# A linear-attention layer with a SiLU MLP: the order of the first chunk's work, the row loads, the bonus sum and the weight transfers rearranged

## The chip, the cores and the metric

The kernel runs on one core of one Trainium2 chip. The metric is the device time of an execution in microseconds. The kernel before took 230.83 us (median of three runs, 230.15 to 231.18). The profile is that of one execution, whose span on the core was 229.3 us.

## The reference

The inputs r, k and v have the shape 4 batches x 8 heads x 768 steps x 48; w and u are 8 x 48. Per batch and head a 48 x 48 state runs over the steps, then an MLP follows:

```python
for t in range(S):
    cur = einsum('bhd,bhe->bhde', u * kt, vt)          # the bonus of the step itself
    y[:, :, t] = einsum('bhd,bhde->bhe', rt, state + cur)
    state = w * state + einsum('bhd,bhe->bhde', kt, vt)
h = x @ w_in                                            # x: y as 3072 x 384; w_in 384 x 2048
return (h * sigmoid(h)) @ w_out                         # w_out 2048 x 384
```

The bonus needs no state: for each step and head it is v times the sum over d of r*u*k.

## The kernel before, in words

The sequence is cut into 6 chunks of 128 steps, and each chunk of each of the 4 batches is a unit: unit i is chunk i // 4 of batch i % 4, 24 units in all. Units 0 to 3 are the first chunk, where the state is zero. A group is the four units of one chunk; the MLP works on a group at a time.

The steps of a unit, by the names of the functions:
- `load` (L69): three transfers (r, k, v) of 192 KB each on the row queue, which SyncE issues. Six buffers of each kind; a load waits until its buffer is free.
- `p1`: TensorE transposes r and k (L211), VectorE multiplies them by powers of w and of 1/w (rT at L213, kT at L215). From unit 4 on ScalarE casts rT to 16 bits (L218).
- `nat_v` (L163): ScalarE casts v to 16 bits (v16).
- `nat_rku` (L169, L171): GpSimd forms ku = k*u and then rku_f = r*ku. `nat_kc` (L175) forms kc, k weighted for the end of the chunk.
- `p2`: TensorE forms the products of kT and rT for the even and odd heads (L225, L227), VectorE multiplies them by the causal mask (am, L232, two instructions).
- The bonus sum over d. In units 0 to 3 it is `bonus_sum` (L193): eight pairs of ScalarE instructions, one pair per head. In the later units it is one VectorE reduction (L181, in `bonus`). GpSimd then forms vu = v * sum (L199, or L184).
- `p3y` and `p3e`: TensorE forms y from am and v16 (L250) and, after the first chunk, from the state (L247); VectorE adds vu (y16, L257).
- `sums` and `state`: TensorE forms the chunk's part of the state from kc and v16 (L266); VectorE copies or adds it (L275 to L280), and GpSimd makes the cast and the decayed copy of it (L282, L284).
- `p4`: TensorE transposes y16 (L298), ScalarE copies it to xT (L299), the input of the MLP.

The MLP is `l1` (three matmuls per tile of 128 hidden columns, L310, then SiLU on ScalarE, L313) and `l2` (four matmuls per part, L322; after four parts VectorE copies the result, L326, and the row queue stores it). An L1 tile is done for all four batches of a group (512 columns of data) or for two of them, a half.

The order on every engine is the order of the program text; there is no planner. `fill(n)` takes MLP tiles off the list `fillers` and places them between the attention steps, to fill TensorE where it would wait. At the start, before any weights are there, `spin(n)` issues n matmuls on a zeroed tile (junk) whose results are not used.

Before units 0 to 3 stand two small vectors: `to_cols` (L120, L123) turns a row of w or u into columns (a transpose and a VectorE copy), VectorE then multiplies up the powers of w (L141 to L145), and `to_rows` (L136, L138) spreads columns over all 128 partitions (four transposes and a ScalarE copy): u_bc, which ku needs, and lamC, which kc needs.

The weights w_in (win, L359) and w_out (wout, L379) come in two transfers each, 768 KB each in the kernel's 16-bit type, issued by GpSimd, between its other instructions.

PSUM tiles are named by tags: `y` has two buffers, shared by spins, y, yT, sps, cols and rows in turn; `tA` has three, for p2 and p1; `moe` three, for the MLP and p1 of units 0 to 3.

Of the kernel before, what the change touches and what calls it, by code (L numbers as in the profile page):

```python
# [8 lines left out]
FP = mybir.dt.float32  # L9
F16 = mybir.dt.float16  # L10
AF = mybir.ActivationFunctionType
# [4 lines left out]
def kernel(  # L16
# [11 lines left out]
    nc = tc.nc  # L28
# [32 lines left out]
    def unit(i):  # L61
        return divmod(i, B)

    def load(i):
        if i >= NU:
            return
        sc, b = unit(i)
        for t, src in ((rin, r), (kin, k), (vin, v)):
            nc.sync.dma_start(out=t[i % NIN][:, :, 0:D],  # L69
                              in_=src[b, :, sc * C:sc * C + C, :]  # L70
                              .rearrange("h t d -> t h d"))
# [3 lines left out]
    wrow = cst.tile([NP, 2, 64], FP)  # L75
    urow = cst.tile([NP, 2, 64], FP)
    junk = cst.tile([128, 512], F16)
    for t, src, q in ((wrow, w, nc.sync), (urow, u, nc.scalar)):
        nc.vector.memset(t[:, :, D:64], 1.0)
        q.dma_start(out=t[:, :, 0:D], in_=bass.AP(tensor=src.tensor, offset=0,  # L80
                                                  ap=[[PW, NP], [D, 2], [1, D]]))
    nc.vector.memset(junk, 0.0)
    for i in range(NIN):
        load(i)
    for t in (rin, kin):
        nc.vector.memset(t[0][:, :, D:64], 0.0)
# [25 lines left out]
    def spin(n):  # L112

        t = ps.tile([128, 512], FP, name="spin", tag="y", bufs=2)
        for _ in range(n):
            nc.tensor.matmul(t, junk[:, 0:128], junk, start=True, stop=True)

    def to_cols(row):
        t = ps.tile([128, 512], FP, name="cols", tag="y", bufs=2)
        nc.tensor.transpose(t[0:PR, 0:NP], row.rearrange("p j d -> p (j d)")[:, 0:PR],  # L120
                            ident[0:NP, 0:NP])
        c = cst.tile([PR, NP], FP, name="cols_sb", bufs=2)
        nc.vector.tensor_copy(out=c, in_=t[0:PR, 0:NP])  # L123
        return c
# [7 lines left out]
    def to_rows(dst, cols):  # L132

        t = ps.tile([128, NP, 2, 64], FP, name="rows", tag="y", bufs=2)
        for p in range(NP):
            nc.tensor.transpose(t[:, p, :, :].rearrange("t j d -> t (j d)")[:, 0:PR],  # L136
                                cols(p), ident[0:PR, 0:PR])
        nc.scalar.copy(out=dst.rearrange("t (p j) d -> t p j d", j=2), in_=t[:, :, :, 0:D])  # L138
# [21 lines left out]
    def nat_v(i):  # L160
        L = live.setdefault(i, {})
        L["v16"] = wrk.tile([128, H, D], F16, name="v16", bufs=6)
        nc.scalar.copy(out=L["v16"], in_=vin[i % NIN])  # L163

    def nat_rku(i):
        n = i % NIN
        L = live.setdefault(i, {})
        ku = wrk.tile([128, H, D], FP, name="ku")
        nc.gpsimd.tensor_tensor(out=ku, in0=kin[n][:, :, 0:D], in1=u_bc, op=ALU.mult)  # L169
        L["rku_f"] = wrk.tile([128, H, D], FP, name="rku_f")  # L170
        nc.gpsimd.tensor_tensor(out=L["rku_f"], in0=rin[n][:, :, 0:D], in1=ku, op=ALU.mult)  # L171

    def nat_kc(i):
        n = i % NIN
        nc.gpsimd.tensor_tensor(out=kc[i % NKC][:, :, 0:D], in0=kin[n][:, :, 0:D],  # L175
                                in1=lamC, op=ALU.mult)

    def bonus(i):
        L = live[i]
        rku = wrk.tile([128, H], FP, name="rku")  # L180
        nc.vector.tensor_reduce(out=rku, in_=L["rku_f"], axis=mybir.AxisListType.X,  # L181
                                op=ALU.add)
        L["vu"] = wrk.tile([128, H, D], FP, name="vu")
        nc.gpsimd.tensor_tensor(out=L["vu"], in0=vin[i % NIN],  # L184
                                in1=rku.unsqueeze(2).broadcast_to([128, H, D]),
                                op=ALU.mult)

    def bonus_sum(i):
        L = live[i]
        L["rku"] = wrk.tile([128, H], FP, name="rku")  # L190
        dump = wrk.tile([128, D], FP, name="dump")
        for h in range(H):
            nc.scalar.activation(out=dump, in_=L["rku_f"][:, h, :], func=AF.Copy,  # L193
                                 accum_out=L["rku"][:, h:h + 1])

    def bonus_vu(i):
        L = live[i]
        L["vu"] = wrk.tile([128, H, D], FP, name="vu")
        nc.gpsimd.tensor_tensor(out=L["vu"], in0=vin[i % NIN],  # L199
                                in1=L["rku"].unsqueeze(2).broadcast_to([128, H, D]),  # L200
                                op=ALU.mult)

    def p1(i, tag="tA"):
        n = i % NIN
        L = live.setdefault(i, {})
        tr = ps.tile([128, NP, C], FP, name="tr", tag=tag, bufs=3)
        tk = ps.tile([128, NP, C], FP, name="tk", tag=tag, bufs=3)
        for t, src in ((tr, rin), (tk, kin)):
            flat = src[n].rearrange("p h d -> p (h d)")
            for p in range(NP):  # L210
                nc.tensor.transpose(t[0:PR, p, :], flat[:, 128 * p:128 * p + PR], ident)  # L211
        L["rT"] = wrk.tile([PR, NP, C], FP, name="rT")
        nc.vector.tensor_tensor(out=L["rT"], in0=tr[0:PR], in1=lamR, op=ALU.mult)  # L213
        L["kT"] = wrk.tile([PR, NP, C], FP, name="kT")
        nc.vector.tensor_tensor(out=L["kT"], in0=tk[0:PR], in1=lamK, op=ALU.mult)  # L215
        if i >= B:
            L["rT16"] = wrk.tile([PR, NP, C], F16, name="rT16")
            nc.scalar.copy(out=L["rT16"], in_=L["rT"])  # L218
# [35 lines left out]
    def p3e(i):  # L254
        L = live[i]
        L["y16"] = wrk.tile([128, H, D], F16, name="y16")
        nc.vector.tensor_tensor(out=L["y16"], in0=L["y"], in1=L["vu"], op=ALU.add)  # L257
# [72 lines left out]
    def l1s(sc, b0=0, b1=B):  # L330
        return [((b1 - b0) / B, lambda ft=ft: l1(sc, ft, b0, b1)) for ft in range(NFT)]

    def l2s(sc, b0=0, b1=B):
        return [(1.0, lambda b=b, part=part: l2(sc, b, part))
                for b in range(b0, b1) for part in range(4)]
# [10 lines left out]

    uT = to_cols(urow)
    to_rows(u_bc, lambda p: uT[:, p:p + 1].broadcast_to([PR, 128]))  # L350
    for s in range(B):
        p1(s, tag="moe")
        nat_v(s)
        nat_rku(s)
        if s:
            bonus_vu(s - 1)
        if s == 2:
            for g in range(2):
                nc.gpsimd.dma_start(  # L359
                    out=win[:, :, 1024 * g:1024 * g + 1024],  # L360
                    in_=moe_w_in[:, 1024 * g:1024 * g + 1024]
                    .rearrange("(q p) n -> p q n", p=128))
        spin(2)
        if s:
            p3y(s - 1)
        p2(s, (lambda: p3e(s - 1)) if s else None)
        spin(2)
        if s:
            p4(s - 1)
        bonus_sum(s)  # L370
        if s == 1:
            to_rows(lamC, lambda p: lamCT[:, p, :])
        spin(2)
    bonus_vu(B - 1)
    p3y(B - 1)
    p3e(B - 1)
    spin(2)
    for g in range(2):
        nc.gpsimd.dma_start(  # L379
            out=wout[:, 8 * g:8 * g + 8, :],  # L380
            in_=moe_w_out[1024 * g:1024 * g + 1024, :].rearrange("(f p) n -> p f n", p=128))
    nat_kc(0)
    nat_kc(1)
    a, b_ = B, B + 1
    nat_v(a)
    nat_rku(a)
    nat_kc(2)
    nat_kc(3)
    for ft in range(4):
        l1(0, ft, 0, 2)  # L390
    p4(B - 1)
# [3 lines left out]
    def front(i):  # L395
        p1(i)
        nat_v(i)
        nat_rku(i)
        nat_kc(i)


    fillers.extend(l1s(0)[4:] + l2s(0))
    for i in range(2):
        sums(i)
        state(i)
        fill(1)
    p1(a)
    fill(1)
    for i in range(2, B):
        sums(i)  # L410
        state(i)
        fill(0.5)
    p2(a)
    bonus(a)
    nat_kc(a)
    fill(2)
    p3y(a)
    sums(a)
    p3e(a)
    state(a)  # L420
    fill(1)
    front(b_)
    fill(1)
    p4(a)
    fill(1)
    p2(b_)
    bonus(b_)
    fill(2)
    p3y(b_)
    sums(b_)  # L430
    p3e(b_)
    state(b_)
    for i in range(NIN):
        load(NIN + i)
    fill(2)
    p4(b_)
    fill(1)
    fillers[0:0] = l1s(1, 0, 2)

    front(B + 2)  # L440
    for i in range(B + 2, NU):
        sc, b = unit(i)
        rate = 1.0
        p2(i)
        fill(2 * rate)
        bonus(i)
        if i + 1 < NU:
            front(i + 1)
        if i >= NIN:
            load(i + NIN)  # L450
        fill(1 * rate)
        p3y(i)
        if sc < NCH - 1:
            sums(i)
        p3e(i)
        if sc < NCH - 1:
            state(i)
        fill(2 * rate)
        p4(i)
        fill(3 * rate)  # L460
        if b == B - 1:
            if sc == 1:
                fillers.extend(l1s(1, 2, 4) + l2s(1))
            else:
                fillers.extend(l1s(sc) + l2s(sc))
# [30 lines left out]
```

## Time and profile before

| engine | busy, us | share of the span |
|---|---|---|
| TensorE matmul | 211.3 | 92% |
| GpSimd | 118.4 | 52% |
| VectorE | 117.2 | 51% |
| ScalarE | 103.5 | 45% |

The shares are means over stages that differ. The profile gives four more views that matter here: busy time by stretch; waits, each with the waiting instruction, the one it waited for, the sum in us, the number and the longest; the timeline, with start, duration, engine, line, operation, output and inputs, and in brackets the idle time before; and the chain of waits, followed back from the last instruction. Matmuls are pipelined, so a group of n has a length of n gaps plus one latency. The releaser of a wait is inferred.

### The profile page before, as it was taken

Reading aid. Unit: us, or ns where it says so; the run is one execution under the profiler, and the core shown is the slowest. Engines: PE = TensorE matmul, PEld = TensorE weight load, DVE = VectorE, ACT = ScalarE, POOL = GpSimd, SP = SyncE. Lnnn points to the kernel's source line nnn. Section 1 sums busy time; section 2 is a strip of 40 time slices with the busy share of each in tenths; the row PEclk is TensorE's granted clock in tenths of the full one; section 3 lists DMA queues with packets and bytes.
Section 4 is the critical chain, followed back from the end, with each engine's and each line's share of the span. In section 5 each row is a group of like instructions: output and inputs, shape, how many; then the busy total and the mean of one; then the engine's idle time right before and its main releaser. Section 6 shows DMA issues by size and latency. Waiting matters only on the chain.

```text
span 229.3 us, 4655 instructions
## 1 busy us (share of the span) xinstructions
PE 211.3 (92%) x1778; PEld 139.3 (61%) x1778; DVE 117.2 (51%) x238; ACT 103.5 (45%) x256; POOL 118.4 (52%) x154
## 2 busy tenths in 40 slices
PE   7698858869789999999999999999999999999993
PEld 2475525455677678677656767666776567654551
DVE  6545534934644585377636656743775365440020
ACT  2355666516473236421488202767213863129500
POOL 8281729965780865574857458625734553410000
PEclk9999999979999999999999999999999999999999
DMA  4997598999940755163762354631012000210011
GB/s 96 214 194 151 87 190 105 188 196 206 175 99 3 172 122 123 37 137 95 168 118 46 64 137 103 137 69 37 36 37 70 3 0 0 71 42 26 3 69 69
DMA packets 81262, 22.32 MB, mean 97 GB/s; under 512 B 75352, under 2 KB 80472, under 8 KB 81240
## 3 DMA queue, kind: packets, MB, share of 16 engines
q1 hardware_dynamic: 78348, 18.88, 37.9%
q0 software_dynamic: 2880, 3.15, 8.8%
q8 instruction: 14, 0.23, 0.4%
q14 instruction: 8, 0.07, 0.1%
q10 hardware_dynamic: 12, 0.00, 0.0%
HBM read 20.45 MB, written 4.72 MB: 110 GB/s over the span
## 4 chain that ended last, share of the span: by engine, by line
PE 74%; POOL 7%; issue 6%; SPq 5%; DVE 3%; ACT 2%; DMA 1%; POOLq 0%; DVEq 0%
PE ops L322 28%; PE hps L310 24%; PE ae L225 9%; SPq L69 5%; PE tr L211 4%; PE tk L211 3%; PE sps L266 2%; POOL kc L175 2%; PE y L250 2%; DMA kin<-in_k_dram 1%; PE yT L298 1%; PE y L247 1%; POOL rku_f L171 1%; ACT gT L313 1%; POOL vu L199 1%
## 5 line engine op out<-in xcount | busy, mean ns | idle before, releaser
L310 PE MATMUL hps<-xT,win 128*128 128x512 f16 (+1 forms) x348 | 71.8, 345 | 3.6 <-ACT gT L313 2.6
L313 ACT ACTIVATE gT<-hps 128x512 f16<-128x512 f32 (+1 forms) x116 | 58.8, 524 | 27.6 <-PE hps L310 25.6
L322 PE MATMUL ops<-wout,gT 128*128 128x384 f16 x384 | 70.0, 326 | 0.0
L184 POOL TENSOR_TENSOR vu<-vin,rku 128x384 f32<-128x384 f32 x20 | 16.6, 830 | 62.5 <-DVE rku L181 62.5
L310 PEld LDWEIGHTS <-win 128*128 128x128 f16 x348 | 32.5, 99 | 27.0 <-issue 5.5
L322 PEld LDWEIGHTS <-gT 128*128 128x128 f16 x384 | 35.8, 98 | 21.4
L232 DVE TENSOR_TENSOR am<-ae,maskM 128x512 f16<-128x512 f32 x24 | 16.6, 692 | 50.5 <-PE ao L227 50.5
L218 ACT CAST rT<-rT 112x512 f16<-112x512 f32 x20 | 12.4, 618 | 50.7 <-DVE rT L213 50.7
L225 PE MATMUL ae<-rT,kT 48*128 48x128 f32 x192 | 28.6, 291 | 1.7 <-DVE kT L215 1.6
L326 DVE COPY osb<-ops 128x384 f32<-128x384 f32 x24 | 13.3, 555 | 33.0 <-PE ops L322 32.5
L225 PEld LDWEIGHTS ae<-rT,kT 48*128 48x128 f32 x192 | 23.9, 193 | 9.1 <-issue 5.9
L227 PE MATMUL ao<-rT,kT 48*128 48x128 f32 x192 | 28.6, 291 | 0.0
L169 POOL TENSOR_TENSOR ku<-kin,u_bc 128x384 f32<-128x384 f32 x24 | 24.1, 1006 | 4.2 <-ACT u_bc L138 4.2
L171 POOL TENSOR_TENSOR rku_f<-rin,ku 128x384 f32<-128x384 f32 x24 | 24.1, 1002 | 1.9
L227 PEld LDWEIGHTS ao<-rT,kT 48*128 48x128 f32 x192 | 23.9, 193 | 0.0
L175 POOL TENSOR_TENSOR kc<-kin,lamC 128x384 f16<-128x384 f32 x24 | 23.9, 1001 | 0.0
L299 ACT COPY xT<-yT 128x384 f16<-128x384 f16 x24 | 11.4, 476 | 24.7 <-PE yT L298 24.7
L213 DVE TENSOR_TENSOR rT<-tr,pi 112x512 f32<-112x512 f32 x24 | 16.6, 690 | 11.3 <-PE tr L211 11.2
L257 DVE TENSOR_TENSOR y<-y,vu 128x384 f16<-128x384 f32 x24 | 13.3, 553 | 7.7 <-POOL vu L199 4.1
L215 DVE TENSOR_TENSOR kT<-tk,pi 112x512 f32<-112x512 f32 x24 | 16.3, 681 | 0.3 <-PE tk L211 0.2
L232 DVE TENSOR_TENSOR am<-ao,maskM 128x512 f16<-128x512 f32 x24 | 16.3, 680 | 0.0
L211 PE MATMUL tk<-ident,kin 128*112 128x128 f32 x96 | 15.3, 285 | 0.0
(62 smaller groups left out, 224.9 us busy)
## 6 DMA issues: line engine op xcount, KB each, us to landing
rin<-in_r_dram SPq DMA_DIRECT2D x24, 192.0 KB, 2.9
kin<-in_k_dram SPq DMA_DIRECT2D x24, 192.0 KB, 3.6
vin<-in_v_dram SPq DMA_DIRECT2D x24, 192.0 KB, 3.6
out_dram<-osb SPq DMA_DIRECT2D x24, 192.0 KB, 1.9
win<-in_moe_w_in_dram POOLq DMA_DIRECT2D x2, 768.0 KB, 9.0
wout<-in_moe_w_out_dram POOLq DMA_DIRECT2D x2, 768.0 KB, 9.8
wrow<-in_w_dram SPq DMA_DIRECT2D x1, 1.5 KB
urow<-in_u_dram ACTq DMA_DIRECT2D x1, 1.5 KB
```

The lines of the kernel that those rows point to most:

```text
L169: nc.gpsimd.tensor_tensor(out=ku, in0=kin[n][:, :, 0:D], in1=u_bc, op=ALU.mult)
L171: nc.gpsimd.tensor_tensor(out=L["rku_f"], in0=rin[n][:, :, 0:D], in1=ku, op=ALU.mult)
L175: nc.gpsimd.tensor_tensor(out=kc[i % NKC][:, :, 0:D], in0=kin[n][:, :, 0:D], in1=lamC, op=ALU.mult)
L184: nc.gpsimd.tensor_tensor(out=L["vu"], in0=vin[i % NIN], in1=rku.unsqueeze(2).broadcast_to([128, H, D]), op=ALU.mult)
L211: nc.tensor.transpose(t[0:PR, p, :], flat[:, 128 * p:128 * p + PR], ident)
L213: nc.vector.tensor_tensor(out=L["rT"], in0=tr[0:PR], in1=lamR, op=ALU.mult)
L225: nc.tensor.matmul(ae[:, p, :], L["kT"][0:D, p, :], L["rT"][0:D, p, :], start=True, stop=True)
L227: nc.tensor.matmul(ao[:, p, :], L["kT"][64:PR, p, :], L["rT"][64:PR, p, :], start=True, stop=True)
L232: nc.vector.tensor_tensor(out=am, in0=a, in1=maskM.unsqueeze(1).broadcast_to([128, NP, C]), op=ALU.mult)
L310: nc.tensor.matmul(hps, win[:, q, ft * 128:(ft + 1) * 128], xts[sc][:, q, b0:b1, :].rearrange("p b t -> p (b t)"), start=(q == 0), stop=(q ...
L313: nc.scalar.activation(out=gts[sc][:, ft, b0 * C:b1 * C], in_=hps, func=AF.Silu)
L322: nc.tensor.matmul(ops, gts[sc][:, ft, b * C:(b + 1) * C], wout[:, ft, :], start=(ft == 0), stop=(ft == NFT - 1))
```

## The change

It does five things.

1. The row of u is no longer loaded from ScalarE's queue. The row queue now carries w, then r and k of unit 0, then u, then v of unit 0. Unit 0's transposes are put ahead of u's `to_cols` and `to_rows`, which run between rT and kT of unit 0 (the argument `mid` of `load` and of `p1`).
2. The bonus sum of units 0 to 3 goes from ScalarE to one VectorE reduction, as in the later units, placed after the masks of the unit. `nat_rku` is split into `nat_ku` and `nat_rk`, and vu of the unit before is placed between them on GpSimd. y16 of the unit before is placed ahead of both masks, not between them.
3. The first weight matrix comes in three transfers (512, 512 and 1024 columns), the second in two as before, and kc of unit 0 goes ahead of the latter. Two groups of spins change in number, and one at the end of units 0 to 3 is gone.
4. Units 4 and 5 are ordered anew: their v16 cast is placed behind SiLUs, the state sums of units 0 to 3 are spread among their steps, and the bonus is placed earlier.
5. The list of fillers for this stretch holds only group 0's L1 tiles; the halves of group 1 and group 0's L2 parts are appended afterwards, and two places to fill are put before unit 6's p2.

The diff, cut to its core:

```diff
+    load_row(wrow, w)
+    load(0, mid=lambda: load_row(urow, u))
+    for i in range(1, NIN):
         load(i)
...
     def bonus_sum(i):
         L = live[i]
         L["rku"] = wrk.tile([128, H], FP, name="rku")
-        dump = wrk.tile([128, D], FP, name="dump")
-        for h in range(H):
-            nc.scalar.activation(out=dump, in_=L["rku_f"][:, h, :], func=AF.Copy,
-                                 accum_out=L["rku"][:, h:h + 1])
+        nc.vector.tensor_reduce(out=L["rku"], in_=L["rku_f"], axis=mybir.AxisListType.X,
+                                op=ALU.add)
...
         nc.vector.tensor_tensor(out=L["rT"], in0=tr[0:PR], in1=lamR, op=ALU.mult)
+        if mid:
+            mid()
...
-    uT = to_cols(urow)
-    to_rows(u_bc, lambda p: uT[:, p:p + 1].broadcast_to([PR, 128]))
+    def to_cols_u():
+        t = to_cols(urow)
+        spin(1)
+        to_rows(u_bc, lambda p: t[:, p:p + 1].broadcast_to([PR, 128]))
+
     for s in range(B):
-        p1(s, tag="moe")
+        p1(s, tag="moe", mid=to_cols_u if s == 0 else None)
         nat_v(s)
-        nat_rku(s)
+        nat_ku(s)
         if s:
             bonus_vu(s - 1)
+        nat_rk(s)
         if s == 2:
-            for g in range(2):
-                nc.gpsimd.dma_start(
-                    out=win[:, :, 1024 * g:1024 * g + 1024], ...
+            for c0, c1 in ((0, 512), (512, 1024), (1024, 2048)):
+                nc.gpsimd.dma_start(out=win[:, :, c0:c1], ...
-        spin(2)
         if s:
             p3y(s - 1)
-        p2(s, (lambda: p3e(s - 1)) if s else None)
+            p3e(s - 1)
+        spin(3)
+        p2(s)
+        bonus_sum(s)
         spin(2)
         if s:
             p4(s - 1)
-        bonus_sum(s)
...
     bonus_vu(B - 1)
     p3y(B - 1)
     p3e(B - 1)
-    spin(2)
+    nat_kc(0)
     (the two transfers of the second weight matrix)
-    nat_kc(0)
-    nat_kc(1)
-    nat_v(a)
-    nat_rku(a)
-    nat_kc(2)
-    nat_kc(3)
+    nat_ku(a)
+    nat_rk(a)
+    for i in range(1, B):
+        nat_kc(i)
     (L1 tiles 0 to 3 in halves, with unit 3's p4 between, as before)
...
-    fillers.extend(l1s(0)[4:] + l2s(0))
+    fillers.extend(l1s(0)[4:])
```

The order of units 4 and 5 after that, with a = 4 and b = 5, was: sums and state of 0 and 1, each with a fill; p1(a); sums and state of 2 and 3; p2(a), bonus(a), kc(a); p3y(a), sums(a), p3e(a), state(a); p1, v16, ku, rk and kc of b; p4(a); p2(b), bonus(b); p3y(b), sums(b), p3e(b), state(b); p4(b); with 14 fills among them. It is now:

```
p1(a) fill(1) v16(a) sum(a) vu(a) sums+state(0) fill(1) p2(a) fill(1) sums+state(1) fill(1)
p3y(a) p3e(a) kc(a) sums+state(2) fill(1) sums+state(3) p1(b) ku(b) rk(b) fill(1) p4(a)
sums+state(a) fill(1) p2(b) sum(b) vu(b) kc(b) fill(2) v16(b) fill(1) p3y(b) p3e(b)
sums+state(b) (loads of units 6 to 11) fill(2) p4(b) p1(6) ... fill(2)
```

The loop over units 6 to 23 is as before, but for y16 being placed ahead of the state sums in the text.

More of the change, by code (lines that the diff above doesn't have):

```diff
@@ L62, in unit, with load @@
         return divmod(i, B)
-    def load(i):
+    def load(i, mid=None):
         if i >= NU:
@@ L68, in load @@
         for t, src in ((rin, r), (kin, k), (vin, v)):
+            if t is vin and mid:
+                mid()
             nc.sync.dma_start(out=t[i % NIN][:, :, 0:D],
@@ L77, with load_row @@
     junk = cst.tile([128, 512], F16)
-    for t, src, q in ((wrow, w, nc.sync), (urow, u, nc.scalar)):
+    nc.vector.memset(junk, 0.0)
+    for t in (wrow, urow):
         nc.vector.memset(t[:, :, D:64], 1.0)
[L80 to L83, printed above, removed]
+    def load_row(t, src):
+        nc.sync.dma_start(out=t[:, :, 0:D], in_=bass.AP(tensor=src.tensor, offset=0,
+                                                        ap=[[PW, NP], [D, 2], [1, D]]))
+    load_row(wrow, w)
+    load(0, mid=lambda: load_row(urow, u))
+    for i in range(1, NIN):
         load(i)
@@ L163, in nat_v, with nat_ku, nat_rk @@
         nc.scalar.copy(out=L["v16"], in_=vin[i % NIN])
-    def nat_rku(i):
-        n = i % NIN
+    def nat_ku(i):
         L = live.setdefault(i, {})
-        ku = wrk.tile([128, H, D], FP, name="ku")
-        nc.gpsimd.tensor_tensor(out=ku, in0=kin[n][:, :, 0:D], in1=u_bc, op=ALU.mult)
+        L["ku"] = wrk.tile([128, H, D], FP, name="ku")
+        nc.gpsimd.tensor_tensor(out=L["ku"], in0=kin[i % NIN][:, :, 0:D], in1=u_bc,
+                                op=ALU.mult)
+    def nat_rk(i):
+        L = live[i]
         L["rku_f"] = wrk.tile([128, H, D], FP, name="rku_f")
-        nc.gpsimd.tensor_tensor(out=L["rku_f"], in0=rin[n][:, :, 0:D], in1=ku, op=ALU.mult)
+        nc.gpsimd.tensor_tensor(out=L["rku_f"], in0=rin[i % NIN][:, :, 0:D], in1=L["ku"],
+                                op=ALU.mult)
     def nat_kc(i):
@@ L176, in nat_kc @@
                                 in1=lamC, op=ALU.mult)
[L178 to L186, printed above, removed]
     def bonus_sum(i):
@@ L201, in bonus_vu, with p1 @@
                                 op=ALU.mult)
-    def p1(i, tag="tA"):
+    def p1(i, tag="tA", mid=None):
         n = i % NIN
@@ L213, in p1 @@
         nc.vector.tensor_tensor(out=L["rT"], in0=tr[0:PR], in1=lamR, op=ALU.mult)
+        if mid:
+            mid()
         L["kT"] = wrk.tile([PR, NP, C], FP, name="kT")
@@ L345, in fill @@
             f()
-    uT = to_cols(urow)
-    to_rows(u_bc, lambda p: uT[:, p:p + 1].broadcast_to([PR, 128]))
+    def to_cols_u():
+        t = to_cols(urow)
+        spin(1)
+        to_rows(u_bc, lambda p: t[:, p:p + 1].broadcast_to([PR, 128]))
     for s in range(B):
-        p1(s, tag="moe")
+        p1(s, tag="moe", mid=to_cols_u if s == 0 else None)
         nat_v(s)
-        nat_rku(s)
+        nat_ku(s)
         if s:
             bonus_vu(s - 1)
+        nat_rk(s)
         if s == 2:
-            for g in range(2):
-                nc.gpsimd.dma_start(
-                    out=win[:, :, 1024 * g:1024 * g + 1024],
-                    in_=moe_w_in[:, 1024 * g:1024 * g + 1024]
-                    .rearrange("(q p) n -> p q n", p=128))
-        spin(2)
+            for c0, c1 in ((0, 512), (512, 1024), (1024, 2048)):
+                nc.gpsimd.dma_start(out=win[:, :, c0:c1],
+                                    in_=moe_w_in[:, c0:c1]
+                                    .rearrange("(q p) n -> p q n", p=128))
         if s:
             p3y(s - 1)
-        p2(s, (lambda: p3e(s - 1)) if s else None)
+            p3e(s - 1)
+        spin(3)
+        p2(s)
+        bonus_sum(s)
         spin(2)
@@ L397, in front @@
         nat_v(i)
-        nat_rku(i)
+        nat_ku(i)
+        nat_rk(i)
         nat_kc(i)
-    fillers.extend(l1s(0)[4:] + l2s(0))
[L403 to L406, printed above, removed]
+    fillers.extend(l1s(0)[4:])
     p1(a)
     fill(1)
[L409 to L412, printed above, removed]
-    p2(a)
-    bonus(a)
-    nat_kc(a)
-    fill(2)
-    p3y(a)
+    nat_v(a)
+    bonus_sum(a)
+    bonus_vu(a)
+    sums(0)
+    state(0)
+    fill(1)
+    p2(a)
+    fill(1)
+    sums(1)
+    state(1)
+    fill(1)
+    p3y(a)
+    p3e(a)
+    nat_kc(a)
+    sums(2)
+    state(2)
+    fill(1)
+    sums(3)
+    state(3)
+    p1(b_)
+    nat_ku(b_)
+    nat_rk(b_)
+    fill(1)
+    p4(a)
     sums(a)
-    p3e(a)
     state(a)
     fill(1)
-    front(b_)
-    fill(1)
[L424 to L428, printed above, removed]
+    p2(b_)
+    bonus_sum(b_)
+    bonus_vu(b_)
+    nat_kc(b_)
+    fill(2)
+    nat_v(b_)
+    fill(1)
     p3y(b_)
+    p3e(b_)
     sums(b_)
-    p3e(b_)
     state(b_)
@@ L436 @@
     p4(b_)
-    fill(1)
-    fillers[0:0] = l1s(1, 0, 2)
+    fillers.extend(l1s(1, 0, 2) + l2s(0))
     front(B + 2)
+    fill(2)
     for i in range(B + 2, NU):
         sc, b = unit(i)
-        rate = 1.0
         p2(i)
-        fill(2 * rate)
-        bonus(i)
+        fill(2)
+        bonus_sum(i)
+        bonus_vu(i)
         if i + 1 < NU:
@@ L450 @@
             load(i + NIN)
-        fill(1 * rate)
+        fill(1)
         p3y(i)
+        p3e(i)
         if sc < NCH - 1:
             sums(i)
-        p3e(i)
-        if sc < NCH - 1:
             state(i)
-        fill(2 * rate)
+        fill(2)
         p4(i)
-        fill(3 * rate)
+        fill(3)
         if b == B - 1:
```

## The prediction

> **What bounds the kernel now.** I read the busy times by stretch first, then the waits inside the stretches that are not full, then single lines of the timeline. The stretches (columns: start and end, length, then busy us and count for TensorE, its weight loads, VectorE, ScalarE, GpSimd, then granted TensorE clock, DMA share, GB/s):
>
> ```profile
> 14.00:31.50 17.50, 14.15 (x142) 9.42 (x141) 10.26 (x17) 9.48 (x48) 8.11 (x9) 1.00 0.80 145
> 31.50:60.40 28.90, 22.57 (x182) 14.62 (x181) 15.45 (x35) 15.45 (x41) 20.59 (x24) 0.94 1.02 176
> 60.40:75.00 14.60, 13.50 (x142) 10.87 (x143) 7.36 (x14) 7.46 (x22) 7.82 (x10) 1.00 0.40 81
> 75.00:200.00 125.00, 124.83 (x1125) 84.57 (x1123) 71.25 (x136) 55.56 (x112) 72.26 (x86) 1.00 0.35 81
> ```
>
> From 75 us on TensorE has no gap (124.83 of 125), so nothing that the change does there can gain. All it can win lies before 75: in the first 31.5 us (the attention of units 0 to 3, a chain of latencies in which spins fill TensorE) and from 31.5 to 60.4, where TensorE is busy 22.57 of 28.9 us at clock 0.94. The waits of 31.5 to 75, then of the first 31.5 us, say who makes it wait:
>
> ```profile
> POOL vu L199 <- ACT dump L193: 4.4, 1, 4.4
> DVE y L257 <- POOL vu L199: 4.1, 1, 4.1
> PEld L266 <- POOL kc L175: 3.7, 4, 1.9
> PE hps L310 <- ACT gT L313: 2.4, 3, 1.8
> PE sps L266 <- POOL kc L175: 2.2, 2, 1.8
> ```
>
> ```profile
> POOL vu L199 <- ACT dump L193: 7.2, 3, 5.1
> DVE rT L213 <- PE tr L211: 4.4, 4, 2.0
> POOL ku L169 <- ACT u_bc L138: 4.2, 1, 4.2
> PE rows L136 <- DVE cols_sb L123: 1.9, 1, 1.9
> ```
>
> ScalarE's bonus sum (dump) is what GpSimd waits for in every unit of the first chunk: 11.6 us in four waits. Behind vu stand, on GpSimd's queue, the weight transfers and kc; behind y16 stands the last transpose that the MLP needs. Single lines of the timeline (start, duration):
>
> ```profile
> 16.67 0.37 PE L225 MATMUL ae<-rT,kT 48*128 48x128 f32 x1 [0.31 <-DVE kT L215]
> 17.86 0.69 DVE L232 TENSOR_TENSOR am<-ae,maskM 128x512 f16<-128x512 f32 x1 [1.25 <-PE ao L227]
> 33.75 0.83 POOL L199 TENSOR_TENSOR vu<-vin,rku 128x384 f32<-128x384 f32 x1 [4.38 <-ACT dump L193]
> 36.13 1.47 PE L310 MATMUL hps<-xT,win 128*128 128x256 f16 x12 [0.57 <-ACT xT L299]
> 48.04 0.54 PE L266 MATMUL sps<-v,kc 128*112 128x96 f16 x4 [1.84 <-POOL kc L175]
> 60.40 0.37 PE L225 MATMUL ae<-rT,kT 48*128 48x128 f32 x1 [1.01 <-DVE kT L215]
> ```
>
> The last is p2 of unit 6, my yardstick: when it starts, TensorE has done units 4 and 5, twelve whole L1 tiles of group 0 and two L2 parts (1.3 us). In the new order it will have done the same, with four half L1 tiles (4 x 0.33 = 1.3 us) in place of the two parts. So the shift of this instruction is the gain.
>
> **What the skill says.** "TensorE: Matmul & The Clock Gate", Part 1: half clock by default, full clock after one busy window of about 3.4 us, half again after an idle one, windows free-running. The trace agrees in kind: f32 matmul pairs come every 0.21 us until 13.3 and every 0.11 us from 16.9; after the 1.84 us gap at 48.04 four transposes take 0.85 us instead of 0.44, until about 51.7. "DMA: Bandwidth & Descriptors", "Issuing engines are not separate DMA queues": another issuing engine saves only sequencer time. Here the u issue costs ScalarE 1.24 us at 0.81, with nothing waiting behind it, so moving it is worth nothing by itself. "GPSIMD Engine Reference", 4.1: a sum along the free axis belongs on VectorE; the trace: 0.54 us there (L181) against 8 pairs every 0.367 = 2.9 us on ScalarE (11.89 to 14.80 for unit 0).
>
> **Part by part.** *u third on the row queue, inside p1(0).* Before, TensorE did cols(u) at 6.0 and waited 1.9 us for its copy, which stood behind the powers of w on VectorE (ending 8.02); only then rows (8.15) and unit 0's transposes (8.95). Now the transposes follow the second five spins at 6.0 and end by 7.75 (0.215 each at half clock); rT 8.02 to 8.71, cols copy 0.15, kT to 9.5 (before 11.59). Rows start 8.95. Before, no landing times are shown for the first loads; r issued at 1.71 with the median 2.9 lands at 4.6, k at 2.37 + 3.6 = 6.0, u in v's old place (2.99 + 3.6 = 6.6) before 7.75. Nothing waits by this. v moves one issue (0.65 us) and has room until 9.6.
> Clock: TensorE is now busy from 1.2 to 8.35, so by the skill full clock comes at 8 at the latest instead of 13.6. If so, rows, spin(3) and p2(0) run fast and the first mask product (am) starts at 11.3; if not, rows 0.85, spins 1.28 and p2 with its 2.12 to am put it at 13.2 (before 13.76). The bounds on this are 0 and 1.9 us; since no row shows the landings, I take the middle, 0.95.
>
> *Bonus sum on VectorE.* Adds 4 x about 0.5 us to VectorE, takes 2.9 us per unit off the chain. Stage now: rT and kT 1.29, to p2 0.05, p2 to am 1.20 (16.67 to 17.86), two am 1.22, sum 0.46: 4.2 us from rT to rT, VectorE-bound; before 5.7 and 5.0 (15.33, 21.05, 26.04). GpSimd needs per stage ku 1.0 + vu 0.83 + rk 1.0 = 2.9, hidden. y16(s-1) lies under p2(s): vu is ready 0.95 after the sum, before kT ends. Spins (3 + 2 + 2, 1.5 us) lie in TensorE's waits. Stage 1 adds 0.5 for the rows of lamC.
> With the later clock: first am 13.2, sum to 14.9, rT at 14.9, 19.65, 23.9; the last am ends 27.7, sum 28.2, vu(3) 28.25 to 29.05, y16(3) at 29.1. Three weight issues (3 x 0.85) on GpSimd at 21.1 to 23.7 hold vu(2), and so y16(2), by 0.4 us; counted. From y16 to the second group of L1 halves was 34.61 to 36.13 = 1.52: they start at 30.62 against 36.13, 5.5 us earlier.
>
> *Weights in 3 + 2.* First L1 now needs only 512 columns. Issued at 19.3 to 21.1; the 768 KB piece took 7.6 us to land, so the small one lands between 4.8 (an estimate: the fixed 2 us that "DMA: Bandwidth & Descriptors", Anatomy of one DMA, gives, plus half of the other 5.6) and 7.6 later: 24 to 28.7, needed 26.3 to 28.2. I take no wait; bound 0 to 2.4. The second piece (needed at 31 to 33) and third (needed by 37) are safe by the 10.4 us of the slower old piece.
>
> *Units 4 and 5 and the states.* After 30.62: halves 1.3, transposes to 32.83; VectorE then runs without a gap: rT, kT to 33.8, sum(4) (product ready 34.0 on GpSimd behind kc(0), two wout issues 1.8, ku, rk) to 34.6, state 0 (four copies, 1.3) to 35.9, am 37.2, state 1 38.5, y16(4) 39.0, states 2 and 3 to 41.6, rT, kT to 42.85, state 4 to 43.5; p2(5) on TensorE 42.9, am 44.1 to 45.4, sum 45.85; GpSimd vu(5) 46.7, kc(5) 47.7. TensorE's sums(5) at 47.75, then two L1 (1.3), yT, transposes of unit 6 (0.88), four halves (1.3): p2(6) at 51.7. Gaps left: 0.85 us at 37.7 (sums(2) wants the PSUM buffer of state 1) and 1.35 us at 46.4 (kc(5)); the wait of p3y(5) for v16(5), now behind two SiLUs, ends at 46.5 inside the latter. 60.40 - 51.7 = 8.7 us. This includes the loss of the old 1.84 us gap and the slow 3.5 us behind it.
>
> *Loads of units 6 to 11* wait for kc(0) (36.3 to 37.3 before, 30.05 at the latest now). Before, from the wout issue at 34.5 to the end of unit 7's k issue (44.05 + 3.56) were 13.1 us; the same from 30.1 gives 43.2, landing by 47, against p1(7) after 51. Hidden.
>
> *Fill after unit 6.* Before, 61.5 to 71 was paced by SiLU: the chain alternates 0.50 of hps with 0.39 of gT. About 12.25 us of TensorE work took 14.6 from 60.4, a loss of 2.35. Four of sixteen halves now come before p2(6), with ScalarE idle. Between 0 and 2.35 saved; I take 0.8.
>
> Sum: 8.7 + 0.95 + 0.8 = 10.45; 230.83 - 10.45 = **220.4 us**.
>
> **Rivals.** *Weights or a late landing at the start* (0.15): the small piece lands in 7.6 us or more because rows of units 4 and 5 (issued to 18.1, DMA share 1.03 in 10 to 20 us) are still moving, or u or k lands after 7.75. Costs 2.4 there, and the 0.95 is gone with a gap at 6: 220.4 + 3.4 = 223.8. For it: 7.6 is the only size shown. Against: the old piece had another beside it.
> *Clock falls in the new gaps* (0.15): 1.35 us idle at 46.4 against 1.84 before, which cost half speed for 3.5 us, 1.8 us of work: 222.2 to 222.5. Against: the 1.77 us gap at 32.6 brought no fall.
> *Gain paid back at the clock* (0.05), the other side: with no early pause TensorE's clock would stay at the 0.94 of 31.5 to 60.4: 6% of 172 us is 10.3, the whole gain, and two more half-speed windows of 1.7 make 234. Against: 1.00 through 150 gapless us.
>
> **How the numbers follow.** The forecast has 0.65. Its own spread: clock 0 to 1.9 (about plus or minus 1), fill 0 to 2.35 (plus 0.8, minus 1.5), so 217.9 to 222.2; waits in a hand-made walk are more likely missed than invented. The upper end takes in both middle rivals: 218 to 225. Faster than 0.5%: forecast and both middle rivals, 0.94; same 0.02; slower 0.04.
>
> **What would show it.** Stages of about 4.2 us between rT starts of units 1 to 3; full clock near 8 us; no L193; second L1 halves near 30; gap before sums(5) about 1.3; p2(6) near 50 to 52; from there TensorE full and everything shifted alike. Wrong if L1 waits for a weight piece, if VectorE's sum stalls on GpSimd's product in each stage, or if units 6 and 7 wait for their rows.

## The result, and the profile after

The changed kernel took 219.49 us (median of four runs, 219.48 to 221.1) against 230.49 us before, a ratio of 0.9539 (95% interval 0.9491 to 0.9586). The forecast was 220.4, with a range of 218 to 225.

The busy times of the changed kernel in four stretches (span 219.4 us; columns as before: start and end, length, busy us and count of TensorE, weight loads, VectorE, ScalarE, GpSimd, clock, DMA share, GB/s):

```profile
0.00:14.00 14.00, 11.10 (x50) 5.85 (x51) 8.32 (x30) 4.07 (x9) 7.79 (x25) 0.88 0.84 167
30.45:52.25 21.80, 18.90 (x170) 12.80 (x169) 14.68 (x34) 12.58 (x27) 19.52 (x24) 1.00 1.09 183
60.00:75.00 15.00, 15.00 (x145) 10.72 (x144) 9.73 (x19) 2.63 (x6) 7.84 (x10) 1.00 0.45 103
75.00:200.00 125.00, 124.83 (x1098) 83.05 (x1096) 67.61 (x127) 57.75 (x115) 66.29 (x79) 1.00 0.31 73
```

The second is the stretch of units 4 and 5, from the second L1 halves to p2 of unit 6. The same stretch in the kernel before:

```profile
36.13:60.40 24.27, 20.61 (x166) 13.34 (x166) 14.89 (x34) 11.35 (x23) 18.20 (x22) 0.93 1.09 186
```

It is 2.5 us shorter. TensorE's idle time in it fell only from 3.7 to 2.9 us; the other 1.7 us are busy time, since a part of the same work ran at half clock before (0.93 on the mean) and none of it does now. TensorE is full from 60 us on, not from about 71. Behind 75 us nothing changed: 124.83 of 125 in both kernels. TensorE's waits from 28 to 75 us in the changed kernel:

```profile
PE sps L267 <- DVE st L281: 1.0, 2, 0.8
PE hps L311 <- ACT gT L314: 0.8, 2, 0.6
PE sps L267 <- POOL kc L186: 0.7, 1, 0.7
PE y L251 <- ACT v L170: 0.4, 1, 0.4
```

The waits for kc fell from 2.2 to 0.7 us and those for SiLU (gT) from 2.4 to 0.8; new are 1.0 us for a PSUM buffer that a state copy holds and 0.4 us for the v16 cast that now stands behind SiLUs. The yardsticks of the prediction, from the timeline:

```profile
13.01 0.69 DVE L233 TENSOR_TENSOR am<-ae,maskM 128x512 f16<-128x512 f32 x1 [3.50 <-PE ao L228]
14.67 0.68 DVE L212 TENSOR_TENSOR rT<-tr,pi 112x512 f32<-112x512 f32 x1
19.51 0.69 DVE L212 TENSOR_TENSOR rT<-tr,pi 112x512 f32<-112x512 f32 x1 [0.56 <-PE tr L210]
23.71 0.68 DVE L212 TENSOR_TENSOR rT<-tr,pi 112x512 f32<-112x512 f32 x1
30.45 1.47 PE L311 MATMUL hps<-xT,win 128*128 128x256 f16 x12 [0.57 <-ACT xT L300]
47.33 0.41 PE L267 MATMUL sps<-v,kc 128*112 128x96 f16 x4 [0.71 <-POOL kc L186]
52.25 0.37 PE L226 MATMUL ae<-rT,kT 48*128 48x128 f32 x1
```

The second L1 halves start at 30.45 (36.13 before), p2 of unit 6 at 52.25 (60.40 before), 8.15 us earlier; the span is 9.9 us shorter, so 1.7 us more come behind p2(6). This is the trace of the execution that took 221.1 us; the other three took 219.5. Where the 1.6 us between them lie, the first experiment shows.

### The profile page after: what moved, and what is told of

It is laid out like the page before. It is cut to its first block, busy times and chain, and to the rows that moved or that the text cites. A ratio compares the mean times of both kernels' runs of the same rounds, so it can differ in the third digit from the quotient of the medians.

```text
span 219.4 us, 4605 instructions
## 1 busy us (share of the span) xinstructions
PE 207.8 (95%) x1781; PEld 137.7 (63%) x1781; DVE 118.5 (54%) x242; ACT 92.7 (42%) x192; POOL 118.9 (54%) x155
## 4 chain that ended last, share of the span: by engine, by line
PE 75%; POOL 7%; DVE 5%; SPq 4%; issue 3%; ACT 2%; DMA 2%; DVEq 0%; POOLq 0%
PE ops L323 29%; PE hps L311 24%; PE ae L226 9%; PE tr L210 4%; SPq L71 4%; PE tk L210 3%; PE sps L267 2%; POOL rku_f L181 2%; DMA vin<-in_v_dram 2%; PE y L251 1%; PE yT L299 1%; PE y L248 1%; POOL vu L198 1%; DVE rT L212 1%; POOL ku L175 1%
## 5 line engine op out<-in xcount | busy, mean ns | idle before, releaser
L311 PE MATMUL hps<-xT,win 128*128 128x512 f16 (+1 forms) x348 | 70.5, 342 | 1.5 <-ACT gT L314 0.9
L198 POOL TENSOR_TENSOR vu<-vin,rku 128x384 f32<-128x384 f32 x24 | 19.9, 829 | 64.5 <-DVE rku L192 63.0
L311 PEld LDWEIGHTS <-win 128*128 128x128 f16 x348 | 32.1, 98 | 24.1 <-issue 2.5
L226 PEld LDWEIGHTS ae<-rT,kT 48*128 48x128 f32 x192 | 23.9, 193 | 9.8 <-issue 7.1
L228 PEld LDWEIGHTS ao<-rT,kT 48*128 48x128 f32 x192 | 23.9, 193 | 0.0
L186 POOL TENSOR_TENSOR kc<-kin,lamC 128x384 f16<-128x384 f32 x24 | 23.9, 999 | 0.0
L123 PE MATMUL spin<-junk 128*128 128x512 f16 x39 | 13.6, 463 | 1.3 <-DVE wrow L82 1.3
```

Source lines behind the costliest of these rows:

```text
L198: nc.gpsimd.tensor_tensor(out=L["vu"], in0=vin[i % NIN], in1=L["rku"].unsqueeze(2).broadcast_to([128, H, D]), op=ALU.mult)
L226: nc.tensor.matmul(ae[:, p, :], L["kT"][0:D, p, :], L["rT"][0:D, p, :], start=True, stop=True)
L228: nc.tensor.matmul(ao[:, p, :], L["kT"][64:PR, p, :], L["rT"][64:PR, p, :], start=True, stop=True)
L311: nc.tensor.matmul(hps, win[:, q, ft * 128:(ft + 1) * 128], xts[sc][:, q, b0:b1, :].rearrange("p b t -> p (b t)"), start=(q == 0), stop=(q ...
```

## Experiments

The kernel before was timed again beside the experiments. Its fastest execution took 228.16 or 228.17 us each time, so times of different experiments are compared directly here.

**The changed kernel again.**

> The changed kernel once more, for a second trace. Clock theory: its shorter executions (219.5 against 221.1) are those in which TensorE keeps full clock through the 1.6 us gap before u's rows, so a trace with span near 217.8 shows p2(0) at full rate and the first mask product near 11.4 instead of 13.0, and a later course that is the same but shifted by 1.6. Rival: the shorter executions save their 1.6 us later, in the fillers or at the row loads, and the first mask product is at 13.0 in them too.

219.49 us (five executions at 219.45 to 219.51, one at 221.07); the trace has the span 217.8. From its timeline, u's rows, the spins behind them and the first mask product; then the first two of these in the trace of 219.4 us shown above:

```profile
9.06 0.57 PE L143 MATMUL rows<-ident,cols_sb 112*128 112x112 f32 x4 [0.92 <-DVE cols_sb L130]
9.47 0.81 PE L123 MATMUL spin<-junk 128*128 128x512 f16 x3
11.40 0.69 DVE L233 TENSOR_TENSOR am<-ae,maskM 128x512 f16<-128x512 f32 x1 [1.89 <-PE ao L228]
```

```profile
9.06 0.62 PE L143 MATMUL rows<-ident,cols_sb 112*128 112x112 f32 x4 [1.64 <-DVE cols_sb L130]
9.48 1.49 PE L123 MATMUL spin<-junk 128*128 128x512 f16 x3
```

Three spins take 0.81 or 1.49 us: TensorE runs at full or at half clock here, and the first mask product comes at 11.40 or 13.01. All later yardsticks are shifted by the same 1.6 us (second halves 28.84, p2(6) 50.63). The clock theory holds, but the gap in front of the rows is not the same in the two traces: 0.92 us where the clock stays, 1.64 us where it falls.

**More spins in front of u's rows.**

```diff
-        spin(1)
+        spin(5)
         to_rows(u_bc, lambda p: t[:, p:p + 1].broadcast_to([PR, 128]))
```

> The changed kernel with five spins instead of one between u's columns and rows (added: four matmuls whose results nobody uses). Clock theory: TensorE is idle for 0.9 instead of 1.6 us before the rows, full clock is not lost again, and all executions take 219.4 or less, none 221.1; the first mask product at 11.4 in every trace. Rival: the fall of the clock does not depend on this gap, and one in six still takes 221; or the spins, if run at half clock, push the rows back and the time rises to 220.

219.41 us, all six between 219.39 and 219.42. With the gap shortened (0.70 us in the trace) no execution takes 221 us. This trace and that of 219.4 us make a close pair, since in both the granted clock became full at 6.0 us. The next two stretches of 3.41 us, first in the trace of 219.4 us, then in this one (columns as above, the clock is the third from the end):

```profile
6.03:9.44 3.41, 1.77 (x14) 1.31 (x13) 3.11 (x8) 1.28 (x4) 0.00 (x0) 1.00 1.04 205
9.44:12.86 3.42, 3.42 (x21) 2.12 (x19) 0.07 (x1) 1.30 (x3) 2.50 (x3) 0.50 1.12 223
```

```profile
6.01:9.42 3.41, 2.71 (x19) 1.67 (x18) 3.10 (x9) 1.28 (x4) 0.00 (x0) 1.00 1.02 202
9.42:12.84 3.42, 3.42 (x32) 2.32 (x30) 1.59 (x4) 1.30 (x3) 2.60 (x3) 1.00 1.02 204
```

This also explains an oddity of the pair above. In the trace where the clock falls, full clock had come earlier (unit 0's eight transposes ended near 7.0 instead of 7.7), but rows are pinned to 9.06 by a copy on VectorE. So the sooner TensorE is quick, the longer it idles, 1.64 against 0.92 us, and then the clock falls back.

The length of the gap is not the whole of it. In the traces of three versions below that keep the single spin, the gap was 1.36 us (the old fillers), 1.45 us (the first weight matrix in two transfers) and 1.53 us (the old order of units 4 and 5), and the clock stayed. In a fourth, the old order inside the stages, it was even 2.23 us, and the spins behind it still ran at full clock:

```profile
9.07 0.57 PE L143 MATMUL rows<-ident,cols_sb 112*128 112x112 f32 x4 [2.23 <-DVE cols_sb L130]
9.47 0.81 PE L123 MATMUL spin<-junk 128*128 128x512 f16 x3
```

In that trace full clock had come at 4.67 us. Where the clock fell in the first 60 us of a trace, it was half for 3.41 us (four traces) or for 6.83 us (one), so it seems to be set anew every 3.41 us. Counted from 4.67, one such step ends at 8.08, inside the gap, and leaves 1.24 us of it in one step and 0.99 us in the next; the gap of 1.64 us lay wholly in one (6.03 to 9.44). That the idle share of a step decides fits this pair, but is not shown: no run moved a gap against the steps on purpose, and a gap of 1.84 us that lay wholly in one step was passed over in a trace below.

**The bonus sum back on ScalarE.**

```diff
-        nc.vector.tensor_reduce(out=L["rku"], in_=L["rku_f"], axis=X, op=ALU.add)
+        dump = wrk.tile([128, D], FP, name="dump")     # units 0 to 3
+        for h in range(H):
+            nc.scalar.activation(out=dump, in_=L["rku_f"][:, h, :], func=AF.Copy,
+                                 accum_out=L["rku"][:, h:h + 1])
```

> The changed kernel with the bonus sum of units 0 to 3 back on ScalarE. Chain theory: a stage becomes sum 2.9 + vu 0.83 + rk 1.0 = 4.8 us on the ScalarE-GpSimd loop against 4.2 to 4.4 on VectorE, so unit 3's y16 comes about 2 us later and the time is 221.5 to 222.5. Rival (order theory): with ku, vu and rk in the new order the ScalarE sum starts right after rk and lies beside the masks, so at most 0.5 us is lost: 219.5 to 220.

224.03 us, 4.5 us more than the changed kernel: the chain theory's direction, but twice its size. Lines of its timeline:

```profile
17.14 0.24 ACT L198 ACTIVATE dump<-rku_f 128x48 f32<-128x48 f32 x1 [1.49 <-POOL rku_f L181]
19.95 0.46 ACT L306 COPY xT<-yT 128x384 f16<-128x384 f16 x1
20.46 0.59 PE L123 MATMUL spin<-junk 128*128 128x512 f16 x2 [2.93 <-ACT xT L306]
21.44 1.06 PE L216 MATMUL tk<-ident,kin 128*112 128x128 f32 x4
```

The expectation looked only at who waits for the sum. Behind it on ScalarE's queue stands the copy of yT to xT, which frees a PSUM buffer; TensorE's next spins wait for that buffer, 2.93 us, unit 2's transposes stand behind the spins, and after the wait they run at half clock (1.06 for four). In the kernel before, the sum stood behind that copy, so this wait is one of this pairing of old sum and new order. How the 4.5 us divide between this wait, the half clock behind it and the wait of vu was not separated: no run puts the copy ahead of the sum in the new order.

**The VectorE sum in the kernel before**, the same edit the other way around, and nothing else.

> The kernel before with this one edit, the bonus sum of units 0 to 3 as one VectorE reduction. Chain theory: vu(1) comes 2.6 us earlier, and unit 3's y16 about 2.5 us earlier, so 227.5 to 228.5. Rival A (the sum is the whole gain of the head): y16(3) 5 us earlier, 225 or less. Rival B (order theory: the old order, with y16 between the masks and vu behind rk, holds the stage): less than 1 us, above 229.5.

226.43 us against 230.84 (ratio 0.9843, 0.9789 to 0.9896), below the range of the chain theory. The medians differ by 4.4 us; the ratio stands for 3.6, since both kernels scatter by about 2 to 3 us. y16(3) came at 32.07 against 34.61, 2.54 us earlier as the chain theory had it, and the second halves at 33.93 (2.2 earlier). In the trace p2(6) was even 4.0 us earlier: the 1.84 us gap before the sums of unit 4 was there as before, but this time without half clock behind it:

```profile
45.70 0.41 PE L264 MATMUL sps<-v,kc 128*112 128x96 f16 x4 [1.84 <-POOL kc L175]
46.59 0.60 PE L209 MATMUL tr<-ident,rin 128*112 128x128 f32 x4
```

The same transposes took 1.06 in the kernel before. So some 1.8 us of these 4.0 are the clock and not the sum. At the start the clock worked the other way: half up to 16.4 us here, up to 14.0 in the trace of the kernel before, and unit 3's rT came 0.34 us later; from there to y16(3) the sum saved 2.9 us.

**The old order inside the stages of units 0 to 3**, with the sum on VectorE.

```diff
-        if s:
-            bonus_vu(s - 1)
         nat_rk(s)
+        if s:
+            bonus_vu(s - 1)
...
-            p3e(s - 1)
         spin(3)
-        p2(s)
-        bonus_sum(s)
+        p2(s, (lambda: p3e(s - 1)) if s else None)
         spin(2)
         if s:
             p4(s - 1)
+        bonus_sum(s)
```

> The changed kernel with the old order inside the stages of units 0 to 3 (vu of the unit before behind rk on GpSimd, y16 of the unit before between the two masks), but the sum still on VectorE. Order theory: y16 between the masks adds 0.5 us to VectorE's chain of each stage and holds back the transpose of y and so the next unit's transposes on TensorE: periods of 4.8 to 5.2 instead of 4.2 to 4.8, 1.5 to 2.5 us in all: 221 to 222. Rival: with the sum off ScalarE the order is indifferent, since VectorE has the same work: within 0.4 us of 219.5.

221.62 us, all within 0.02: 2.1 us slower. Periods from rT to rT are 5.7 and 5.0 us (13.07, 18.79, 23.78) against 4.8 and 4.2, and in each of the three stages TensorE waits 0.7 us for y16; the first two:

```profile
16.81 0.34 PE L299 MATMUL yT<-ident,y 128*128 128x128 f16 x3 [0.71 <-DVE y L258]
22.53 0.34 PE L299 MATMUL yT<-ident,y 128*128 128x128 f16 x3 [0.70 <-DVE y L258]
```

These periods are those of the kernel before (15.33, 21.05, 26.04), and with the VectorE sum in the kernel before they were no shorter (15.41, 21.39, 26.38). So the sum alone does not shorten the stage; it takes its 2.5 us off the end, where unit 3's y16 waits for it. Nor does the new order alone: with the sum on ScalarE it had periods of 8.9 and 5.4 us (12.81, 21.68, 27.11). It takes both. The edit moves vu and y16 at once, and which of the two counts was not separated.

**u's part undone.**

```diff
-    load(0, mid=lambda: load_row(urow, u))
+    nc.scalar.dma_start(out=urow[:, :, 0:D], in_=(u, as in the kernel before))
+    load(0)
...
-        p1(s, tag="moe", mid=to_cols_u if s == 0 else None)
+        p1(s, tag="moe")          # and u's to_cols and to_rows ahead of the loop, without spin
```

> The changed kernel with u's part undone: u on ScalarE's queue, its columns and rows ahead of unit 0's transposes. Chain theory: the first mask product comes at 13.8 as in the kernel before, 0.7 to 2 us later than in the changed kernel by the state of the clock, and all behind it shifts: 220.2 to 221.5. Rival: GpSimd's ku and rk of unit 0 set the pace, and u_bc comes 0.4 us earlier here, so no loss or a small gain: 219 to 219.6.

221.07 us, 1.6 us slower. rows wait 1.96 us again, unit 0's transposes start at 8.94 instead of 5.8, the first mask product comes at 12.83, earlier than expected, since full clock came at 11.0 us in this trace and at 14.0 in that of the kernel before. The chain theory holds; that u_bc is ready earlier buys nothing.

**The first weight matrix in two transfers.**

```diff
-            for c0, c1 in ((0, 512), (512, 1024), (1024, 2048)):
+            for c0, c1 in ((0, 1024), (1024, 2048)):
```

> The changed kernel with the first weight matrix in two transfers of 1024 columns. Weights theory: the first piece lands 7.6 us after its issue near 19.2, at 26.8, and the first L1 half (at 26.2 in the trace of 217.8 us) waits up to 0.7 us; but y16(3) holds the second halves in any case, so at most 0.3 us is lost, and GpSimd saves one issue of 0.8 us: 219.2 to 219.8. Rival: the pieces are needed, since a landing near 30 us would hold both groups of halves: 221 or more.

220.3 us (219.94 to 221.08), 0.8 us slower, more than the 0.3 expected; in the trace, which is that of the fastest execution, 0.5. The wait is there and has the size expected of it, but y16(3), which comes when it did, does not cover all of it: unit 3's transpose of y stands behind the late halves on TensorE, and the second halves start at 29.40 against 28.84.

```profile
27.08 1.49 PE L311 MATMUL hps<-xT,win 128*128 128x256 f16 x12 [0.75 <-DMA win<-in_moe_w_in_dram]
29.40 1.47 PE L311 MATMUL hps<-xT,win 128*128 128x256 f16 x12 [0.67 <-ACT xT L300]
```

**The old fillers**, everything else as changed.

```diff
-    fillers.extend(l1s(0)[4:])
+    fillers.extend(l1s(0)[4:] + l2s(0))
...
-    fillers.extend(l1s(1, 0, 2) + l2s(0))
+    fill(2)
+    fillers[0:0] = l1s(1, 0, 2)
     front(B + 2)
-    fill(2)
```

> The changed kernel with only the filler list as before: L2 parts of group 0 fill ahead of unit 6, and the sixteen halves of group 1 come together behind its p2. Pacing theory: SiLU then paces the halves, and the 1.7 us that the changed kernel gains behind p2(6) are lost: 221.0 to 221.4. Rival: these 1.7 us come from other waits (row loads, kc) and the time stays within 0.3 us of 219.5; or L2 parts placed at 48 us wait for the second weight matrix (landing near 44) and it costs more.

221.35 us (median; two of six at 222.9, with a granted clock of 0.992 where the others have 0.997 to 1.000), 1.9 us slower. p2(6) starts at 50.77 against 50.63, so all of it is lost behind. The halves come in one run of sixteen and are paced by SiLU; the sets of twelve take 1.8 us instead of 1.5:

```profile
51.87 1.79 PE L311 MATMUL hps<-xT,win 128*128 128x256 f16 x12
56.29 1.77 PE L311 MATMUL hps<-xT,win 128*128 128x256 f16 x12 [0.50 <-ACT gT L314]
```

**The old order of units 4 and 5**, with the old fillers. The edit puts back the block from unit 4's ku to unit 6, as listed under the change.

> The changed kernel with the old order of units 4 and 5 and the old filler list. If the order itself is worth what the walk gave (gaps before the sums, and the half-clock stretch behind the 1.84 us gap), 24.3 us from the second halves to p2(6) instead of 21.8, and 1.7 us behind it: 223.2 to 223.8. Rival: the half-clock stretch was chance, and without it the old order takes 22.5 (as in the kernel before with the VectorE sum): 221.5 to 222.2.

223.66 us (single executions from 221.99 to 225.27), 4.2 us slower, of which 1.9 are the fillers. The old gap and the half clock behind it are back:

```profile
40.75 0.61 PE L267 MATMUL sps<-v,kc 128*112 128x96 f16 x4 [1.84 <-POOL kc L186]
42.43 1.06 PE L210 MATMUL tr<-ident,rin 128*112 128x128 f32 x4
```

From the second halves (28.83) to p2(6) (52.91) it takes 24.1 us, as in the kernel before (24.3); the new order takes 21.8. Most of the 2.3 us beside the fillers is the clock. The single execution at 222.0 had a granted clock of 1.000; the four near 223.6 had 0.991 or 0.992, and that at 225.3 had 0.985. So without half clock the old order costs 0.6 us (222.0 against 221.35), as the rival had it, and the half clock, which five of six executions met, costs 1.7 us. No trace of the execution at 222.0 was kept.

**kc ahead of vu in the kernel before**, the gap alone.

```diff
-    bonus(a)
     nat_kc(a)
+    bonus(a)
```

> The kernel before with one edit, kc(4) ahead of vu(4) on GpSimd, so that the 1.84 us wait of TensorE for kc(4) shrinks to about 0.3. If the wait costs its length and the half clock behind it (1.9 us more), 227.0 to 227.8; if the wait alone, 229.2; if TensorE catches up in the fillers behind it, no change.

227.75 us against 230.07 (ratio 0.9913, 0.9877 to 0.9949). In its trace the wait is 0.23 us and p2(6) starts at 57.03, 3.4 us earlier, of which 0.3 come from before the second halves. So wait and half clock together cost 3.1 us in the trace. The medians differ by 2.3 and the ratio stands for 2.0 (1.2 to 2.8), between the wait alone (1.6) and both, as they should if only some executions of the kernel before lose the clock there; that share was not measured.

**A version with both gaps shortened**: the five spins, and for unit 5 what the last experiment does for unit 4.

```diff
-        spin(1)
+        spin(5)
...
-    bonus_vu(b_)
     nat_kc(b_)
-    fill(2)
-    nat_v(b_)
+    bonus_vu(b_)
     fill(1)
+    nat_v(b_)
+    fill(2)
```

> The changed kernel with the five spins, with kc(5) ahead of vu(5) on GpSimd and the v16 cast of unit 5 one filler earlier. It should end the waits of sums(5) for kc(5) (0.7 us) and of y(5) for v16(5) (0.4 us) on TensorE, which has no slack from there on: 218.2 to 218.5 against 219.4. Rival: vu(5) comes 0.8 us later, so y16(5) and the state of unit 5 take the place of the waits and nothing is gained.

218.38 us (218.37 to 218.41), 1.1 us less than the changed kernel, 1.0 less than with the five spins alone, and the lowest of all; ratio to the kernel before 0.9504 (0.9471 to 0.9537). The wait for kc is 0.24 us and that for v16 is gone; y16(5) did not take its place.

## Why the prediction was right

**What bounds.** That only the time before 75 us could give anything held: 124.83 of 125 us busy behind it in both kernels.

**Stages of 4.2 us.** Forecast rT at 14.9, 19.65, 23.9 and second halves at 30.62, for the later clock; measured 14.67, 19.51, 23.71 and 30.45 in the trace that has that clock. The periods, forecast at 4.75 in stage 1 and 4.2 behind it, were measured at 4.84 and 4.20, and the chain named for them was right: rT, kT, the products, the masks and the sum follow each other, with VectorE waiting only 0.6 to 0.8 us at a time for TensorE. What the prediction put under the heading of the sum rests on two things by the experiments, the sum on VectorE and the order inside the stage: undoing the order alone costs 2.1 us, and the sum without the order gives 2.5 us at y16(3) and no shorter stage.

**u and the clock.** Forecast for the first mask product: 11.3 or 13.2, measured 11.40 or 13.01. That full clock would come by 8 us, as the Trainium skill, "TensorE: Matmul & The Clock Gate", Part 1, has it, is borne out: the spins still take 0.43 each up to 5.8, and unit 0's transposes turn quick at about 6 in one trace and 7.5 in the other. The step that failed, in two of ten executions timed, is the next: that the clock, once up, stays through the gap in front of rows. The working itself had that gap (spins to 8.35, rows at 8.95) but made it 0.6 us, because it let the spin in front of it run at half clock; it is 0.92 or 1.64. The same part of the page puts half clock behind an idle window of about 3.4 us; here a gap of 1.64 us was enough in one trace, and the measurement decides. The 0.95 us that the prediction took, the middle of two bounds, is a value that no execution shows: each gains either all 1.6 us of this term or nothing.

**Weights.** No wait, as forecast. The quickest of the three pieces landed after 5.1 us in one trace and 6.8 in the other (forecast for the small ones 4.8 to 7.6); the room was small, since in the second trace the first halves start 7.0 us after the first issue. The 768 KB piece instead would have cost 0.8 us.

**Units 4 and 5.** Sums(5) at 47.33 against a forecast of 47.75, gap for the PSUM buffer 0.77 against 0.85. The gap at unit 5 has another shape: 0.4 for v16(5), which did not lie inside the wait for kc as forecast, then 0.7. p2(6) then came 0.55 us later than forecast; a wait of 0.6 us of the fourth of the four new halves for SiLU would account for it: ScalarE was not idle there, as the prediction had it, but busy with the rT and v16 casts of unit 6.

**Fill behind unit 6.** The term was mis-sized: 0.8 taken, 1.7 measured in the trace and 1.9 by the experiment with the old fillers. The mechanism is the one named, but about three quarters of the loss of 2.35 went, not a third. This accounts for the difference of 0.9 us between 220.4 and 219.5: up to p2(6) the forecast shift was 8.7 + 0.95 = 9.65 and the measured one, in the trace of 217.8 us, 9.77. That these two agree so well is luck: the clock gave about 0.65 us more than the middle value, and units 4 and 5 gave 0.55 us less.

**Rivals.** Weights did not come late. The clock did fall in a gap, but in the one before u's rows and not in the one at 46 us for which the rival was given. Nothing was paid back at the clock behind 75 us.

## What to carry to other kernels

Read what stands behind an instruction on its own queue, not only who waits for its result: the sum on ScalarE, put back, cost 4.5 us instead of the 2 to 3 expected, and the trace shows TensorE waiting 2.9 us for the copy behind it. Where an engine without slack follows a stretch of latencies, put what it waits for first on the feeding engine (kc ahead of vu), and spread work that a second engine paces. Treat a gap of TensorE of about 1.6 to 1.8 us as possibly costing its length again, as it did here in some executions and not in others, and when two bounds are states and not sizes, forecast one of them and not the middle.

## What the runs showed of the hardware

A gap of the same 1.84 us was followed by half clock in two kernels (four transposes in 1.06 us) and not in a third (0.60). In the changed kernel, a gap of 1.64 us in front of u's rows went with half clock and a time of 221.1 us, and one of 0.92 us with full clock and a time of 219.5; in another version a gap of 2.23 us at the same place passed without half clock. A fall of the clock cost 1.6 to 1.8 us where it could be told apart. What decides beyond the length of the gap stays open; that it matters where the gap lies in steps of 3.41 us fits the traces in part. Spins whose results nobody uses are worth their place for this alone: four more of them took the spread from 1.6 us to 0.03.
